# Reload order, head 0's loads first, and key sums on VectorE in a fused linear and softmax attention kernel

## The chip, the cores and the metric

The kernel runs on one core of a Trainium2 chip. The core has five engines that run their own instruction streams and meet only through semaphores: TensorE (PE: matmuls; PEld is its weight load), VectorE (DVE), ScalarE (ACT), GpSimd (POOL) and SyncE (SP, here only an issuer of DMAs). Data lie in DRAM, in SBUF (128 partitions, on the chip) and in PSUM, eight banks of 128 x 512 float32 into which TensorE writes its sums. VectorE and ScalarE read banks; GpSimd works on SBUF tiles alone. DMAs are issued from a queue of SP, of ACT or of POOL. The metric is the device time in microseconds, lower is better.

## The reference

One input x (2048 tokens, width 1024) goes through two attention blocks, and a gate per token mixes their outputs:

```python
x = A_x
g = _sigmoid((x * gate_w).sum(-1, keepdims=True))
a = _A_ref(x, A_wqkv, A_wo)
b = _B_ref(x, B_wqkv, B_wo)
return g * a + (1 - g) * b
```

Block A is linear attention with 32 heads of width 32. With `phi(t) = where(t > 0, t + 1, exp(t)) + 1e-6` it needs for each head the sum over tokens of `phi(k)` times v (`kv`), the plain sum of `phi(k)` over tokens (`z`), and then `phi(q) kv / (phi(q) z)`. Block B is softmax attention with 32 heads of width 32: `softmax(q k / sqrt(32)) v`. Each has its own q, k, v weights (1024 x 3072) and output weights (1024 x 1024).

## The kernel before

**Precision.** Matmul operands are cut into a high part (ScalarE rounds a copy to fp32r) and a low part (the rest, a subtraction). A product is then three matmuls: high x high, high x low, low x high (`three`, L150 to L159). One matmul of 512 columns takes a slot of 0.2275 us in the planner's table.

**First half, products for block B.** The tokens are handled in two halves, J = 0 and J = 1. For each, v's weights are applied first (`v_pass`), then a block of A's keys and B's values (`block`), then eight *quads* (`quad`, f = 0 to 7), each of which makes q or k for two groups of four heads by seven products (a Strassen-like scheme; `PRODUCTS` s = 0 to 6, four blocks of three matmuls each). The cut weights of the quads go round a ring of 13 places in the big tiles 14 to 20; product s of quad f uses entry (7 f + s) modulo 13. For J = 0 the ring is

```python
spots("20a 20b 15a 14a 19a 19b 17b 14b 18a 18b 16a 16b 17a")
```

A quad gives its side work one step after each product: the step behind product s is written out behind that product and ahead of product s + 1. The weights of the next quad are cut in these steps (ScalarE copies at L304, VectorE subtractions at L299).

**v's cut weights** of the first half are stored to DRAM (`wv_d`) and loaded again for J = 1 into the eight places `STARTS[1]` = 19a 19b 17b 18a 18b 14b 16a 16b (k = 0 to 7). `reload_wv` (L822) does this for k = 0 to 5, one per step, from the step behind product 1 of quad 6 on; `change` does k = 6 and 7 in quad 7. Each is two DMAs of 256 KB on ScalarE's queue (L820). ScalarE's stream is in order, so a DMA that waits holds up the copies behind it.

**The heads' stacks.** Scores of block B use stacked operands: a queries' tile (`q_first` for the first 512 tokens, `q_rest` for the other 1536) and a keys' tile (`k_stack`, 2048 tokens). Their rows 0 to 95 are three loads of 32 rows (high, high, low and high, low, high); rows 96 to 127 are set to zero, with ones in two rows of the keys. Heads 0 and 1 are loaded at the end of the first half: `leave` (steps of the last quad of J = 1) calls `load_first`, with the DMAs on POOL's queue and the memsets on POOL. The order is: first block of queries and keys of head 0 (behind product 3), the same of head 1 (behind product 4), then behind product 6 the rest of head 0, and the rest of head 1.

**The main stretch.** From about 563 us on a planner writes one order out by hand. It keeps an estimate of each engine's time (`T`) and picks among four streams: `linear` (block A: units of 24 matmuls; kinds `kv` with 48 units, `q` with 32, `o` with 32), `maxima` (all scores once, VectorE takes the row maxima at L1440), `heads_` (scores again, ScalarE takes the exponentials at L1579, then the product with v at L1726) and `output`. The order on each engine is fixed when the kernel is built; on the chip the engines only wait for each other's semaphores. Banks are taken and given back in the same plan, so a matmul waits for the last reader of its bank.

- *A kv unit* (L1307 on): ScalarE takes v (L1315) and makes the exponentials and the rest (`phi`, L1098 to L1100); `more`, put off to VectorE, joins them into the key features (L1321) and so frees the unit's bank; GpSimd adds the features, 128 x 256, to `zsum` (L1324, L1326), which both lie in SBUF.
- *Weights of the next kind*: `renew` puts a weight block in `next_w`; `split_w` makes the high part on ScalarE (L1047) and the low part, 128 x 512 from two SBUF tiles, on the engine that it is given (L1049), GpSimd.
- *Softmax sums* on GpSimd: it adds the exponentials of a head, 1536 columns at a time or 512 (L1657, L1661); VectorE does the remaining 512 columns in a bank (L1677).
- *The gate*: `gate_step` (L735) asks for a block of x on SyncE's queue, ScalarE scales it (L753) 8 us later by the plan, GpSimd adds it (L759); at the end VectorE turns the sums into the gate (L771 to L773).

SyncE's stream holds nearly all other DMAs, in order: stores of q and k of the quads, the gate's x, v of a head (`load_v`, L1415), and x for the units (`load_half`).

Of the kernel before, what the change touches and what calls it, by code (L numbers as in the profile page):

```python
# [20 lines left out]
DH = 32  # L21
# [29 lines left out]
def kernel(  # L51
# [18 lines left out]
    nc = tc.nc  # L70
    D, S = xT.shape
    H = D // DH
    NK = D // P
    HK = NK // 2
    NT = S // P
    NJ = S // C
# [6 lines left out]
    def f32(ap):  # L83
        return ap.bitcast(F32)
# [46 lines left out]
    zsum = [mid[6][:, i * HC:(i + 1) * HC] for i in range(2)]  # L131
# [31 lines left out]
    def use(eng, cost, *after):  # L163

        T[eng] = max(T[eng], *after, 0.0) + cost
        return T[eng] + LATENCY[eng]
# [14 lines left out]
    def defer(fn, at, cost=0.6, rank=1, prev=None):  # L181
        item = Later(fn, at, cost, rank, prev)
        later.append(item)
        return item
# [86 lines left out]
    def give(b, at=0.0, items=()):  # L271

        held[b] = False
        free[b] = max(free[b], at)
        readers[b].extend(items)

    def both(*times):

        return None if None in times else max(times)
# [39 lines left out]
    KH = NK // 2  # L319
# [462 lines left out]
    def beside(*streams):  # L782

        streams = list(streams)
        while True:
            for s in list(streams):
                next(s, None)
            yield
# [29 lines left out]
    def load_wv_again(k):  # L818
        for p in range(2):
            nc.scalar.dma_start(f32(ring_w(v_ring(1, k), p)), wv_d[k][:, p * C:(p + 1) * C])  # L820

    def reload_wv():  # L822

        for _ in range((QUADS - 2) * NP + 1):
            yield
        for k in range(NK - 2):
            load_wv_again(k)
            yield

# [150 lines left out]
    def split_kv(raw, k):  # L980
        split(wpart(k, 0), wpart(k, 1), raw, nc.vector)
# [4 lines left out]
    def leave():  # L986

        split_kv(raw_a[2], 2)
        split_kv(raw_a[3], 3)
        yield  # L990
        split_kv(raw_a[0], 0)
        split_kv(raw_a[1], 1)
        yield
        for k in range(KH, NK):
            split_kv(raw_b[k - KH], k)
            if 0 < k - KH < 3:
                load_first(k - KH - 1, 0)
            yield
        load_first(0, 1)
        load_first(1, 1)  # L1000

    def load_first(h, part):

        if not part:
            load_q(h, 0, now=nc.gpsimd)
            load_k(h, 0, nc.gpsimd)
        else:
            load_q(h, 1, NJ, nc.gpsimd)
            for j in range(1, NJ):
                load_k(h, j, nc.gpsimd)  # L1010

    T["sp"] = 0.0

# [40 lines left out]
    next_w = deque()  # L1054

    def pump_w(now=False):

        while next_w and (now or coming_w and coming_w[0][1] <= T["pe"]):
            follow, k, mark, eng = next_w.popleft()
            if not coming_w:  # L1060
                more_w(True)
            split_w(*follow, k, *coming_w.popleft(), eng)
            mark.end = w_ready[k]
            if k + LEAD_W < NK:
                later_w.append((*follow, k + LEAD_W))
            more_w(now)
        more_w(now)
# [76 lines left out]
    def keys_alone(n):  # L1144

        while kv_todo and kv_todo[0][0] <= n:
            yield lambda: both(kv_todo[0][1](), bank_at()) if kv_todo else 0.0
            if kv_todo and kv_todo[0][0] <= n:
                use("pe", AV_SWITCH, kv_todo[0][1]())
                keys_now(T["pe"])  # L1150
# [53 lines left out]
    z_end = [0.0, 0.0]  # L1204
# [39 lines left out]
    def linear():  # L1244
        extra = iter(())
        for n, (i, t) in enumerate(units):
            kind, c = chunks[i]
            follow = chunks[i + 1] if i + 1 < len(chunks) else None

            def renew(k):  # L1250

                mark = Later(None, 0.0, 0.0, 0, None)
                w_left[k][:] = [mark]
                next_w.append((follow, k, mark, nc.gpsimd))
                pump_w()

            yield bank_at
# [54 lines left out]
            if kind == "kv":  # L1312
                va = mid[7][:, (n % 2) * HC:(n % 2 + 1) * HC]
                yield from keys_alone(n - 2)
                nc.scalar.copy(va, ps[:, HC:])  # L1315
                use("act", 0.28, T["pe"] + LATENCY["pe"])
                end = phi(ps, e, HC)

                def more(end, c=c, t=t, e=e, ps=ps):
                    pk = e[:, :HC]  # L1320
                    nc.vector.scalar_tensor_tensor(pk, pk, 1.0, ps[:, :HC], op0=ALU.min, op1=ALU.add)  # L1321
                    z_end[c % 2] = use("pool", 0.69, end)
                    if t == 0:
                        nc.gpsimd.tensor_copy(zsum[c % 2], pk)  # L1324
                    else:
                        nc.gpsimd.tensor_add(zsum[c % 2], zsum[c % 2], pk)  # L1326

                todo = [defer(more, end, 0.34)]
                give(b, 0.0, todo)
                keys(n, c, t, e, va, todo)  # L1330
                if t == NT - 1:
                    assert gate_n[0] > NJ * NK
                    extra = chain_of(*(keysum(x) for x in ((0, c) if i == 0 else (c,))))
            elif kind == "q":
                yield from keys_alone(n - 3)
                yield lambda: None if n - 3 not in turned and chunks[units[n - 3][0]][0] == "q" else 0.0
                end = phi(ps, e, C)
                d = dn[n % 2]

                def sums(_, e=e, ps=ps):  # L1340
                    nc.vector.scalar_tensor_tensor(ps, e, 1.0, ps, op0=ALU.min, op1=ALU.add)

                def scaled(_, c=c, ps=ps, r=r):
                    nc.vector.tensor_mul(r, ps, zrep[:, c * C:(c + 1) * C])

                last = []

                def dens(end, r=r, d=d, last=last):
                    nc.vector.tensor_reduce(d, r.rearrange("p (h d) -> p h d", d=DH), AX.X, ALU.add)
                    nc.scalar.add(d, d, eps)  # L1350
                    last[0].at = use("act", 0.2, end)

                def divide(_, t=t, e=e, ps=ps, d=d):
                    nc.vector.reciprocal(d, d)
                    nc.vector.scalar_tensor_tensor(
                        e.rearrange("p (h d) -> p h d", d=DH), ps.rearrange("p (h d) -> p h d", d=DH),
                        g_sb[:, t:t + 1], d.unsqueeze(2).to_broadcast([P, C // DH, DH]),
                        op0=ALU.mult, op1=ALU.mult)

                todo = chain(((sums, 0.63), (scaled, 0.63), (dens, 0.63), (divide, 0.9)), end)  # L1360
                last.append(todo[-1])
                give(b, 0.0, todo)
                tasks.append((lambda todo=todo: None if kv_todo else both(ended(todo + o_left), o_free[(len(turned) + 1) % 2], bank_at()),
                              lambda n=n, c=c, t=t, e=e, todo=todo: queries(n, c, t, e, todo)))
            else:
                res = mid[(7, 10)[n % 2]]
                give(b, use("act", 0.5, T["pe"] + LATENCY["pe"]))
                nc.scalar.copy(res, ps)
                dma(ra_d[t][:, c * C:(c + 1) * C], res)
# [16 lines left out]
    def load_q(h, j, j1=0, now=None):  # L1386

        g, r = divmod(h, 4)
        j1 = max(j + 1, j1)
        q, sl = q_cols(h, j, j1), slice(j * C, j1 * C)  # L1390
        if h < (2 if j else 3):
            nc.gpsimd.memset(f32(q[3 * DH:, :]), 0.0)
        else:
            dma(f32(q[3 * DH:3 * DH + 2, :]), f32(q[3 * DH + 2:3 * DH + 4, :]))
        for b, p in enumerate((0, 0, 1)):
            (now.dma_start if now else dma)(f32(q[b * DH:(b + 1) * DH, :]), qk_d[0][p][g][r * DH:(r + 1) * DH, sl])
        for i in range(j, j1):
            q_ready[h][i] = max(T["pe"] + 8.0, T["sp"] + 5.0)

    def load_k(h, j, now=None):  # L1400

        g, r = divmod(h, 4)
        k = k_stack[h % 2]
        if h < 2 and j == 0:
            nc.gpsimd.memset(f32(k[3 * DH:, :]), 0.0)
            nc.gpsimd.memset(f32(k[3 * DH:3 * DH + 2, :]), 1.0)
        sl = slice(j * C, (j + 1) * C)
        for b, p in enumerate((0, 1, 0)):
            (now.dma_start if now else dma)(f32(k[b * DH:(b + 1) * DH, sl]), qk_d[1][p][g][r * DH:(r + 1) * DH, sl])
        k_ready[h][j] = max(T["pe"] + 6.0, T["sp"] + 4.0)  # L1410

    def v_tile(h):
# [515 lines left out]
    def output():  # L1928
# [55 lines left out]
        for i, (name, n) in enumerate(seq):  # L1984
# [4 lines left out]
            if name == "X21" and n:  # L1989
                load_ra(n + 1)  # L1990

    quad(1, QUADS - 1, beside(leave(), parts))
    assert next(parts, None) is None
    xh_t[2] = sb.tile([P, 2 * HK * P], F32R, name="xh")
    T["sp"] = 0.0
# [124 lines left out]
```

## Time and profile before

| | |
|---|---|
| time, median of three runs | 2838.11 us (2836.34 to 2838.83) |
| the profiled execution: its time, its span | 2837.45 us, 2835.7 us |
| granted TensorE clock, mean | 0.996 |
| busy: PE, DVE, ACT, POOL | 99%, 80%, 59%, 74% |
| busy between 1400 and 1500 us: PE, DVE, ACT, POOL | 99.76, 82.17, 64.01, 97.27 us of 100 |
| largest groups | softmax sums on POOL (L1661) 1641.9 us; maxima on DVE (L1440) 1285.1; exponentials on ACT (L1579) 1156.5 |

How to read it: "PE bank L154 <- DMA big<-wv: 8.0, 1, 8.0" in a list of waits is engine, output and line, who was waited for, then the total in us, the times and the longest. In a timeline a row has the start and the duration in us, the engine ("ACTq" and "SPq" are DMA issues), the line, the operation, output<-inputs and, in brackets, the idle time before and what ended it. A row of windows has the stretch, its length, the busy us of PE, PEld, DVE, ACT and POOL, then TensorE's granted clock, the DMA engines' share and GB/s. In a list of groups the count is followed by busy us, mean ns of one, and the idle time before. A line that gives one source line's instructions has their shortest, median and longest duration in ns.

### The profile page before, as it was taken

The numbers are of one execution on the slowest core, as the hardware profiler recorded it, in microseconds if no ns is written. First come the engines' busy times: TensorE is split into PE (matmuls) and PEld (weight loads), VectorE is DVE, ScalarE is ACT, GpSimd is POOL, SyncE is SP. The second block draws the span as 40 slices with busy tenths as digits, with TensorE's granted clock in tenths as the row PEclk, the third lists the DMA queues.
The fourth block names the chain that finished last, engine by engine and source line by source line (L and its number), as shares of the span: only waits on it lengthen the run. The fifth ranks groups of instructions, "written<-read, shape, count | busy, mean of one in ns | idle before, by whom it ended". The sixth has DMA issues, their size and how long they took to land.

```text
span 2835.7 us, 46700 instructions
## 1 busy us (share of the span) xinstructions
PE 2801.9 (99%) x15784; PEld 2013.6 (71%) x15784; DVE 2267.4 (80%) x3715; ACT 1664.9 (59%) x3167; POOL 2109.6 (74%) x1151
## 2 busy tenths in 40 slices
PE   9998999989999999999999999999999999999999
PEld 8887888876666666676666777676666666676687
DVE  6696759768888888888888877787888888787678
ACT  4333433336676666776666666666767667676622
POOL 0162017468999999999999988998999999999000
PEclk9999999999999999999999999999999999999999
DMA  8587658682443333433334445566544445333774
GB/s 268 174 270 258 202 158 270 222 231 90 103 107 85 86 89 96 114 96 85 85 96 114 142 141 170 172 197 196 168 124 128 128 132 144 101 101 112 261 236 149
DMA packets 391051, 432.77 MB, mean 153 GB/s; under 512 B 105550, under 2 KB 237902, under 8 KB 389020
## 3 DMA queue, kind: packets, MB, share of 16 engines
q1 hardware_dynamic: 366252, 387.69, 45.7%
q0 software_dynamic: 22256, 37.89, 6.2%
q10 hardware_dynamic: 2304, 4.20, 0.4%
q8 instruction: 126, 2.06, 0.3%
q14 instruction: 113, 0.93, 0.1%
HBM read 287.31 MB, written 127.93 MB: 146 GB/s over the span
## 4 chain that ended last, share of the span: by engine, by line
PE 91%; DVE 4%; DMA 3%; ACT 1%; POOL 1%; issue 1%; SPq 0%; ACTq 0%; POOLq 0%; DVEq 0%
PE bank L1726 16%; PE bank L1576 16%; PE bank L1435 15%; PE bank L154 12%; PE bank L157 12%; PE bank L159 12%; PE bank L644 5%; DVE mx L1440 2%; DMA big<-qk 1%; PE bank L1499 1%; ACT big L1579 1%; PE bank L1229 1%; DMA big<-ra 0%; PE bank L1118 0%; DMA big<-big 0%
## 5 line engine op out<-in xcount | busy, mean ns | idle before, releaser
L1661 POOL TENSOR_TENSOR big<-big,big 128x512 f32<-128x512 f32 (+2 forms) x694 | 1641.9, 2370 | 65.4 <-ACT big L1579 19.9
L1440 DVE TENSOR_REDUCE mx<-bank 128x1 f32<-128x512 f32 x2048 | 1285.1, 685 | 282.8 <-PE bank L1435 280.2
L1579 ACT ACTIVATE big<-bank 128x512 f32<-128x512 f32 x2048 | 1156.5, 602 | 349.4 <-PE bank L1576 289.0
L1435 PE MATMUL bank<-big,big 128*128 128x512 f32 x1888 | 743.7, 396 | 13.3 <-DMA big<-qk 7.9
L1576 PE MATMUL bank<-big,big 128*128 128x512 f32 x1888 | 736.2, 396 | 1.0 <-ACT big L1579 0.3
L154 PE MATMUL bank<-big,big 128*128 128x512 f32 x1408 | 552.5, 392 | 10.5 <-DMA big<-wv 8.0
L157 PE MATMUL bank<-big,big 128*128 128x512 f32 x1408 | 551.0, 391 | 0.0
L159 PE MATMUL bank<-big,big 128*128 128x512 f32 x1404 | 549.3, 391 | 1.1 <-DVE big L299 1.1
L1726 PE MATMUL bank<-big,mid 128*32 128x512 f32 x4096 | 454.5, 593 | 0.0
L1576 PEld LDWEIGHTS bank<-big,big 128*128 128x128 f32 x1888 | 353.8, 188 | 125.6 <-issue 45.3
L1435 PEld LDWEIGHTS bank<-big,big 128*128 128x128 f32 x1888 | 355.6, 188 | 101.8 <-DVE mx L1440 12.9
L1726 PEld LDWEIGHTS bank<-big,mid 128*32 128x32 f32 x4096 | 133.4, 110 | 277.4 <-issue 276.0
L154 PEld LDWEIGHTS bank<-big,big 128*128 128x128 f32 x1408 | 265.3, 188 | 71.9 <-DMA big<-wv 8.4
L159 PEld LDWEIGHTS bank<-big,big 128*128 128x128 f32 x1404 | 264.7, 189 | 58.4 <-DVE big L299 2.4
L157 PEld LDWEIGHTS bank<-big,big 128*128 128x128 f32 x1408 | 265.4, 188 | 56.1 <-issue 0.8
L1677 DVE TENSOR_TENSOR bank<-bank,big 128x512 f32<-128x512 f32 x364 | 253.1, 695 | 6.4 <-ACT big L1579 1.4
L304 ACT CAST big<-mid 128x512 fp32r<-128x512 f32 (+1 forms) x169 | 100.2, 618 | 138.6 <-DVE mid L1845 71.7
L299 DVE TENSOR_TENSOR big<-mid,big 128x512 fp32r<-128x512 f32 (+1 forms) x138 | 99.6, 738 | 75.7 <-ACT big L304 75.2
L644 PE MATMUL bank<-big,big 128*128 128x512 f32 x672 | 152.6, 389 | 0.0
L1657 POOL TENSOR_TENSOR big<-big,big 128x1536 f32<-128x1536 f32 (+1 forms) x31 | 132.8, 4285 | 20.4 <-ACT big L1579 20.4
L1734 ACT COPY mid<-bank 128x512 f32<-128x512 f32 x32 | 18.8, 587 | 217.5 <-PE bank L1726 217.5
L644 PEld LDWEIGHTS bank<-big,big 128*128 128x128 f32 x672 | 126.1, 188 | 26.2
(196 smaller groups left out, 2418.9 us busy)
## 6 DMA issues: line engine op xcount, KB each, us to landing
big<-xs SPq DMA_DIRECT2D x202, 256.0 KB
big<-qk SPq DMA_DIRECT2D x690, 64.0 KB
qk<-mid SPq DMA_DIRECT2D x128, 256.0 KB
xh<-xs SPq DMA_DIRECT2D x102, 256.0 KB
big<-oA SPq DMA_DIRECT2D x86, 256.0 KB
xs<-big SPq DMA_DIRECT2D x64, 256.0 KB
oA<-mid SPq DMA_DIRECT2D x64, 256.0 KB
big<-big POOLq DMA_DIRECT2D x50, 256.0 KB, 4.9
```

What stands on the lines that cost most here:

```text
L154: yield nc.tensor.matmul(ps, sh, mh_, start=(kt == 0), stop=False)
L157: yield nc.tensor.matmul(ps, sh, ml_, start=False, stop=(late and last))
L159: yield nc.tensor.matmul(ps, sl, mh_, start=False, stop=last)
L644: nc.tensor.matmul(bank[at + i], x_, w_, start=(kt == u == 0 and not onto), stop=(kt == KH - 1 and u == 2), skip_group_check=onto)
L1435: nc.tensor.matmul(bank[b], q[:, t % TPC * P:(t % TPC + 1) * P], k[:, j * C:(j + 1) * C], start=True, stop=True)
L1440: nc.vector.tensor_reduce(m[:, t, j:j + 1], bank[b], AX.X, ALU.max)
L1576: nc.tensor.matmul(bank[b], k[:, t * P:(t + 1) * P], q_cols(h, j), start=True, stop=True)
L1579: nc.scalar.activation(pr_t[i][:, j * C:(j + 1) * C], bank[b], AF.Exp, scale=SCALE)
L1657: nc.gpsimd.tensor_add(lacc[:, :qp], pr(0)[:, :qp], pr(1)[:, :qp])
L1661: nc.gpsimd.tensor_add(lacc[:, sl], lacc[:, sl], pr(t)[:, sl])
L1677: nc.vector.tensor_add(lacc[:, qp:] if t == NT - 1 else l_b[:, :n], l_b[:, :n], src)
L1726: nc.tensor.matmul(av_b[j * DH:(j + 1) * DH, :], v[:, t, :], pr(t)[:, j * C:(j + 1) * C], start=(t == 0), stop=(t == NT - 1))
```

## The change

Three edits:

1. `reload_wv` takes k in the order 0, 1, 2, 5, 3, 4. Before, k = 3 was written into 18a in the step behind product 4 of quad 6, ahead of product 5, which reads 18a, and k = 4 into 18b ahead of product 6, which reads 18b: these two products read the reloaded blocks. Now each place is written behind the product of quad 6 that reads it.
2. Head 0's queries and keys are loaded as a whole in the step behind product 2 of the last quad, on POOL's queue; head 1's 18 loads are written out behind the quad, on SyncE's queue. The rows 96 to 127 are set behind a tile's loads, for the keys block by block.
3. The key sums (48 instructions) and the low parts of the main stretch's weights (32) go from GpSimd to VectorE. In the plan `more` costs VectorE 0.68 us, in place of 0.34 there and 0.69 on GpSimd; a low part costs 0.6 on VectorE in place of 1.23 on GpSimd.

```diff
-        for k in range(NK - 2):
+        for k in (0, 1, 2, 5, 3, 4):
             load_wv_again(k)
             yield
...
             split_kv(raw_b[k - KH], k)
-            if 0 < k - KH < 3:
-                load_first(k - KH - 1, 0)
+            if k == KH:
+                load_first(0)
             yield
-        load_first(0, 1)
-        load_first(1, 1)
-
-    def load_first(h, part):
-
-        if not part:
-            load_q(h, 0, now=nc.gpsimd)
-            load_k(h, 0, nc.gpsimd)
-        else:
-            load_q(h, 1, NJ, nc.gpsimd)
-            for j in range(1, NJ):
-                load_k(h, j, nc.gpsimd)
+
+    def load_first(h, now=nc.gpsimd):
+        load_q(h, 0, now=now)
+        load_k(h, 0, now)
+        for j in range(1, NJ):
+            load_k(h, j, now)
+        load_q(h, 1, NJ, now)
...
-                next_w.append((follow, k, mark, nc.gpsimd))
+                next_w.append((follow, k, mark, nc.vector))
...
                     nc.vector.scalar_tensor_tensor(pk, pk, 1.0, ps[:, :HC], op0=ALU.min, op1=ALU.add)
-                    z_end[c % 2] = use("pool", 0.69, end)
+                    z_end[c % 2] = end
                     if t == 0:
-                        nc.gpsimd.tensor_copy(zsum[c % 2], pk)
+                        nc.vector.tensor_copy(zsum[c % 2], pk)
                     else:
-                        nc.gpsimd.tensor_add(zsum[c % 2], zsum[c % 2], pk)
-
-                todo = [defer(more, end, 0.34)]
+                        nc.vector.tensor_add(zsum[c % 2], zsum[c % 2], pk)
+
+                todo = [defer(more, end, 0.68)]
...
-        if h < (2 if j else 3):
-            nc.gpsimd.memset(f32(q[3 * DH:, :]), 0.0)
-        else:
+        if h >= (2 if j else 3):
             dma(f32(q[3 * DH:3 * DH + 2, :]), f32(q[3 * DH + 2:3 * DH + 4, :]))
         for b, p in enumerate((0, 0, 1)):
...
+        if h < (2 if j else 3):
+            nc.gpsimd.memset(f32(q[3 * DH:, :]), 0.0)
...
-        if h < 2 and j == 0:
-            nc.gpsimd.memset(f32(k[3 * DH:, :]), 0.0)
-            nc.gpsimd.memset(f32(k[3 * DH:3 * DH + 2, :]), 1.0)
...
+        if h < 2:
+            nc.gpsimd.memset(f32(k[3 * DH:, sl]), 0.0)
+            nc.gpsimd.memset(f32(k[3 * DH:3 * DH + 2, sl]), 1.0)
...
     quad(1, QUADS - 1, beside(leave(), parts))
+    load_first(1, nc.sync)
     assert next(parts, None) is None
```

## The prediction

> **What bounds the kernel now.** First the page's busy times, then the waits of PE.
>
> ```profile
> span 2835.7 us, 46700 instructions
> PE 2801.9 (99%) x15784; PEld 2013.6 (71%) x15784; DVE 2267.4 (80%) x3715; ACT 1664.9 (59%) x3167; POOL 2109.6 (74%) x1151
> PE bank L154 <- DMA big<-wv: 8.0, 1, 8.0
> PE bank L1435 <- DMA big<-qk: 7.9, 2, 7.5
> PE bank L1435 <- DVE mx L1440: 3.4, 1, 3.4
> ```
>
> TensorE is busy for 2801.9 of 2835.7 us. An edit can win only at its pauses, and three of these make 19 us. It can lose wherever it makes TensorE wait. The change touches the first pause with its reloads, the second with its loads, and with its third edit it gives work to VectorE in a stretch where TensorE and VectorE run hand in hand.
>
> **Edit 1, the order of v's reloads.** The view is the timeline around 262 us and the windows beside it.
>
> ```profile
> 257.77 0.98 ACTq L820 DMA_DIRECT2D big<-wv  x2
> 262.52 0.80 PE L154 MATMUL bank<-big,big 128*128 128x512 f32 x1 [7.99 <-DMA big<-wv]
> 264.68 0.63 PE L157 MATMUL bank<-big,big 128*128 128x512 f32 x1
> 265.11 0.63 PE L159 MATMUL bank<-big,big 128*128 128x512 f32 x1
> 268.16 0.69 DVE L513 TENSOR_TENSOR mid<-bank,mid 128x512 f32<-128x512 f32 x1 [7.76 <-PE bank L159]
> 262.00:333.00 71.00, 70.48 (x299) 57.76 (x300) 41.96 (x65) 26.52 (x46) 0.00 (x0) 0.96 0.74 231
> ```
>
> L513 evaluates product 5 of a quad, so the pause stands ahead of product 5, in quad 6 (the next-to-last quad of the first half, J = 0). Its ring place is 18a: index 6 x 7 + 5 = 47, modulo 13 gives 8, and entry 8 of the first ring is 18a. v's fourth reload (k = 3) goes to 18a, too, and is written out one step earlier, behind product 4. (k = 4 and product 6 stand the same way with 18b.) So the product has to wait for that reload: issued at 257.77, it lets TensorE go at 262.52. With the new order the step behind product 4 loads k = 5 into 14b, which product 4 itself was the last to read; 18a follows behind product 5 and 18b behind product 6. No product reads a reloaded place any more, and the 7.99 us go. Behind the pause the matmuls start 0.43 us apart (264.68, 265.11). The mean clock of 0.96 over 71 us means 0.04 x 71 / 0.5 = 5.7 us at half speed, in which 2.8 us are lost; these go as well. What is late next: ScalarE issues these DMAs in order with its copies, as before; v's first reloaded weights are read only after seven more products, and 18a's DMA now waits for a product that ends before ScalarE gets there. **-10.8 us**; at worst 8.0, should the transfers crowd together.
>
> [...]
>
> **Edit 2, the loads of heads 0 and 1.** The second pause is named after a DMA of qk; the weight load of the same matmul names another releaser.
>
> ```profile
> PEld bank L1435 <- DVE mid L1321: 7.9, 1, 7.9
> 587.63 0.72 ACT L753 ACTIVATE mid<-mid,omg_sb 128x512 f32<-128x512 f32 x1 [11.24 <-DMA mid<-in_xT]
> 590.83 0.45 ACT L1100 ACTIVATE bank<-bank,eps 128x256 f32<-128x256 f32 x1
> 591.31 0.42 DVE L1321 SCALAR_TENSOR_TENSOR mid<-mid,bank 128x256 f32<-128x256 f32 x1 [9.32 <-ACT bank L1100]
> 591.79 0.80 PE L1435 MATMUL bank<-big,big 128*128 128x512 f32 x1 [7.46 <-DMA big<-qk]
> 566.06 0.45 SPq L171 DMA_DIRECT2D mid<-in_xT  x1
> 567.45 6.96 SPq L171 DMA_DIRECT2D xh<-xs  x2
> 576.36 2.70 SPq L171 DMA_DIRECT2D mid<-in_xT  x3
> 577.70 1.46 POOL L1396 DMA_DIRECT2D big<-qk  x3
> 570.00:592.00 22.00, 14.47 (x93) 11.39 (x93) 3.26 (x8) 5.72 (x13) 12.04 (x21) 0.92 1.08 246
> ```
>
> The chain is: x for the gate, asked for by SyncE at 576.36, lets ScalarE's L753 start at 587.63; behind it in ScalarE's order stands L1100; then VectorE's L1321 empties a bank; the bank is free at 591.73, and TensorE goes on at 591.79. Head 0's queries and keys are not in this chain, so their earlier arrival wins nothing. Head 1's 18 loads, 12 of which GpSimd issued from 577.70 on, now stand on SyncE's queue ahead of the gate's x. At 0.45 us each (row at 566.06) they put its issue back by 8.1 us. Against this, those 12 loads (nine of 64 KB, three of 192 KB: 1.15 MB) no longer share the DMA engines, which are full in this stretch (share 1.08); at 246 GB/s that is 4.7 us. The memsets, split by blocks, stay on GpSimd, which has nothing waiting for it there. **+3.4 us**, between -4.7 (only the sharing counts) and +8.1 (only the issue counts).
>
> **Edit 3, key sums and low parts on VectorE.** The groups by form between 660 and 1570 us, POOL's and then DVE's:
>
> ```profile
> L1661 POOL TENSOR_TENSOR big<-big,big 128x1536 f32<-128x1536 f32 x150 | 526.1, 3507 | 9.6
> L1661 POOL TENSOR_TENSOR big<-big,big 128x512 f32<-128x512 f32 x178 | 227.9, 1287 | 10.9
> L1657 POOL TENSOR_TENSOR big<-big,big 128x1536 f32<-128x1536 f32 x14 | 59.3, 4235 | 0.0
> L1326 POOL TENSOR_TENSOR mid<-mid,mid 128x256 f32<-128x256 f32 x36 | 29.3, 813 | 6.8 <-ACT big L1579 6.8
> L1049 POOL TENSOR_TENSOR big<-big,big 128x512 fp32r<-128x512 f32 x14 | 17.8, 1290 | 0.0
> L1049 POOL TENSOR_TENSOR big<-mid,big 128x512 fp32r<-128x512 f32 x7 | 8.9, 1290 | 0.0
> L1324 POOL COPY mid<-mid 128x256 f32<-128x256 f32 x2 | 0.8, 395 | 0.0
> L1440 DVE TENSOR_REDUCE mx<-bank 128x1 f32<-128x512 f32 x964 | 597.5, 684 | 135.5 <-PE bank L1435 135.1
> L1321 DVE SCALAR_TENSOR_TENSOR mid<-mid,bank 128x256 f32<-128x256 f32 x38 | 15.8, 415 | 4.1 <-ACT bank L1100 2.1 <-PE bank L154 1.7
> ```
>
> 36 + 2 + 21 = 59 instructions go from POOL to DVE here. By themselves they take 38 x 0.42 (as L1321) + 21 x 0.69 (as L513) = 30 us there, and VectorE idles 135.5 us ahead of its maxima. That idle time hides them, and the planner is told of them (0.68 and 0.6 us); without the cover they would cost the 30.
>
> But all 59 have no operand in a bank. What such VectorE instructions do beside a busy GpSimd is seen in two other places:
>
> ```profile
> 243.54 1.67 POOL L695 TENSOR_TENSOR big<-zrep,big 128x512 fp32r<-128x512 f32 x1
> 244.19 1.57 DVE L490 TENSOR_TENSOR mid<-mid,mid 128x512 fp32r<-128x512 f32 x1
> 653.25 3.48 POOL L1657 TENSOR_TENSOR big<-big,big 128x1536 f32<-128x1536 f32 x1
> 656.81 10.50 POOL L1661 TENSOR_TENSOR big<-big,big 128x1536 f32<-128x1536 f32 x3
> 655.18 1.58 DVE L771 TENSOR_SCALAR g_sb<-g_sb 128x16 f32<-128x16 f32 x1
> 656.80 0.25 DVE L772 RECIPROCAL g_sb<-g_sb 128x16 f32<-128x16 f32 x1
> 657.09 3.19 DVE L773 TENSOR_SCALAR omg_sb<-g_sb 128x16 f32<-128x16 f32 x1
> L490 DVE TENSOR_TENSOR mid<-mid,mid x64: 676/692/2446, 138.2 to 565.0; 128x512 fp32r<-128x512 f32 x64
> ```
>
> L490 has a median of 692 ns; met by GpSimd's L695 (over at 245.21) it takes 1.57 us and ends at 245.76, 0.55 later. L771 ends at 656.76, 0.03 after GpSimd's L1657; L773 ends at 660.28, where the first of the three L1661 (3.5 us each) ends at 660.31. So a VectorE instruction whose inputs all lie in SBUF stands until GpSimd's running one is over. L1321 and the maxima, which read a bank, show nothing of it.
>
> [...]
>
> How much is it? GpSimd is busy almost throughout. An instruction that comes at a random moment meets each kind with its share of the 910 us and then waits half its length: (526.1 x 3.507 + 227.9 x 1.287 + 59.3 x 4.235) / 2 / 910 = 1.31 us; 59 of them 77 us. What passes on to TensorE is read off L771 and L773: beyond 0.25 each (L772) they lost 4.27 us and TensorE waited 3.4, so 0.9 was cushioned. With the first 0.9 us of each wait free, the mean left is, by kinds, 0.578 x 2.607^2 / 7.014 + 0.250 x 0.387^2 / 2.574 + 0.065 x 3.335^2 / 8.47 = 0.66 us; 59 x 0.66 = 39. GpSimd loses 57 us of its 910 and is met 6% less often: -2. Eleven more low parts come after 1570 us, where VectorE has more room; I take +3 of at most 7 (11 x 0.66). The nine key sums before 653 meet little: 0. **+40 us.** Ends: no cushion, 77 + 7 = +84; all absorbed and GpSimd's relief worth something, -5, about what TensorE idles in the eight windows of 100 us from 700 to 1500 (4.4 us; the first and the last of them):
>
> ```profile
> 700.00:800.00 100.00, 99.88 (x681) 66.06 (x683) 84.16 (x147) 68.20 (x134) 96.30 (x52) 1.00 0.44 112
> 1400.00:1500.00 100.00, 99.76 (x652) 64.22 (x644) 82.17 (x144) 64.01 (x126) 97.27 (x45) 1.00 0.33 86
> ```
>
> I take the value that goes by L773, the one place in which this very collision reached TensorE. What is queued behind a standing VectorE instruction are the maxima, for whose banks TensorE waits.
>
> **The sum.** -10.8 + 3.4 + 40 = +32.6 us. The profiled run took 2837.45 us (1.75 beyond its span); that gives **2870 us**. The median of the runs shown, 2838.11, lies 0.7 above that run, which I leave inside the range.
>
> **Rivals.**
> *VectorE's idle time swallows the waits* (faster). For: it idles 135.5 us there, 77 us of waits fit in as a total, and the planner puts the new work where it thinks VectorE idle. Against: the idle time comes in pieces, and TensorE was passed 3.4 of 4.27 us. It decides if the cushion reaches about 3.5 us, the common long GpSimd instruction. Then edit 3 is 0: 2837.45 - 10.8 + 3.4 = **2830**. Chance 0.17.
> *The waits cancel edit 1* (no change). If four fifths of the new instructions fall on GpSimd's 178 short ones, a wait is 0.64 us on average, under the cushion, and a fifth of the 39 is left: 8 us. 2837.45 - 10.8 + 3.4 + 8 = **2838**. Chance 0.11.
> *Edit 1 doesn't do what it says*, since ScalarE issues the new order late enough for another product to wait: 2870 + 10.8 = **2881**. Chance 0.05; for the index sum above is plain.
> *Forecast*: **2870**, own range 2846 to 2908 (the upper end has edit 3 at +78, nearly without cushion). Chance 0.67.
>
> **How the numbers follow.** About 0.2% (5.7 us) is what a measurement of this kernel can tell from no change. Slower: 0.67 + 0.05 = 0.72; within: 0.11; faster: 0.17. The range runs from 2826, under the faster rival, to 2908; outside are 0.06 above (no cushion at all) and 0.05 below.
>
> **What the profile after would show.** Edit 1: no wait for wv in PE's list, and no clock below 1 near 260 us. Edit 2: L753's wait for in_xT about 3 us longer, and the bank's release by L1321 with it. Edit 3: the key sums and low parts on DVE at means near 1.6 and 1.9 us instead of 0.4 and 0.7, many ending with a POOL instruction; PE waits for DVE's maxima by the dozen. I am wrong if those means stay under 0.8 us, or if they are long and PE's waits don't grow.

## The result and the profile after

The changed kernel takes **2945.65 us** (median of four runs, 2945.42 to 2950.07) against 2838.47 us for the kernel before on the same chip: a ratio of 1.0383, 95% interval 1.0365 to 1.0401, or 107.2 us more. In the changed file the lines of the main stretch have moved up by 5: the maxima are L1435 (their matmul L1430), the exponentials L1574 (matmul L1571), the join of the key features L1316, the key sums L1319 and L1321, the low parts L1044, GpSimd's running sums L1656 and its first sum of a head L1652.

The page of the changed kernel, its busy times and its chain:

```profile
span 2943.6 us, 46715 instructions
...
PE 2858.7 (97%) x15784; PEld 2023.1 (69%) x15784; DVE 2395.0 (81%) x3795; ACT 1669.1 (57%) x3167; POOL 2036.3 (69%) x1065
...
PE 83%; DVE 12%; issue 1%; ACT 1%; DMA 1%; POOL 1%; SPq 0%; DVEq 0%; POOLq 0%; ACTq 0%
```

TensorE was idle for 33.8 us before (2835.7 - 2801.9) and is idle for 84.9 now. Of the chain that ended last, VectorE holds 12%; before it was 4%, by this line of the page of before:

```profile
PE 91%; DVE 4%; DMA 3%; ACT 1%; POOL 1%; issue 1%; SPq 0%; ACTq 0%; POOLq 0%; DVEq 0%
```

The list of TensorE's waits shows who:

```profile
PE bank L1430 <- DVE mx L1435: 32.1, 23, 3.5
PE bank L1571 <- DVE mx L1435: 18.5, 13, 3.3
PE bank L767 <- POOL zrep L759: 6.1, 1, 6.1
PE bank L1571 <- DVE mid L1316: 5.3, 1, 5.3
```

The wait for wv is gone, and 36 waits of the scores' matmuls for VectorE's maxima, 50.6 us, stand where there was one of 3.4. The clock shows the other part. First the row of the changed kernel, then that of before:

```profile
core 0: 2943.6 us, clock 0.986
```

```profile
core 0: 2835.7 us, clock 0.996
```

A mean clock of 0.986 loses 0.014 x 2943.6 = 41 us against full speed, before 0.004 x 2835.7 = 11. So of the 107 us some 30 are TensorE's clock, and 51 are TensorE's visible idle time; what is left, some 26 us, lies inside TensorE's busy time. There the starts of the matmuls lie further apart: summed over the trace, the clock's part and the visible pauses taken out, by some 20 us more than before. Which waits, too short for the list, do this is not shown.

The groups of VectorE between 550 and 1900 us, where all 80 moved instructions lie:

```profile
L1435 DVE TENSOR_REDUCE mx<-bank 128x1 f32<-128x512 f32 x1226 | 767.4, 683 | 147.0 <-PE bank L1430 146.0
...
L1321 DVE TENSOR_TENSOR mid<-mid,mid 128x256 f32<-128x256 f32 x45 | 64.6, 1435 | 1.5
L1044 DVE TENSOR_TENSOR big<-big,big 128x512 fp32r<-128x512 f32 x21 | 41.9, 2000 | 12.9 <-ACT big L1042 12.9
...
L1044 DVE TENSOR_TENSOR big<-mid,big 128x512 fp32r<-128x512 f32 x11 | 15.5, 1409 | 7.2 <-ACT big L1042 7.2
...
L1319 DVE COPY mid<-mid 128x256 f32<-128x256 f32 x3 | 6.5, 2179 | 0.1
```

The moved instructions take 64.6 + 41.9 + 15.5 + 6.5 = 128.5 us. By the shortest of each kind they would take 45 x 0.424, 32 x 0.68 and 3 x 0.29 (293 ns, the shortest copy of e12), 41.7 us. So **87 us** of it is standing. And the maxima still follow 147.0 us of idle time, which has not been used up. Over the whole run that idle time fell by only 20 us, though VectorE is busy for 127.6 us more (2395.0 - 2267.4); first the row of before, then that of the changed kernel:

```profile
L1440 DVE TENSOR_REDUCE mx<-bank 128x1 f32<-128x512 f32 x2048 | 1285.1, 685 | 282.8 <-PE bank L1435 280.2
L1435 DVE TENSOR_REDUCE mx<-bank 128x1 f32<-128x512 f32 x2048 | 1285.9, 685 | 262.8 <-PE bank L1430 260.6
```

One such stand in the changed kernel's timeline, with what it does to TensorE:

```profile
1075.48 10.63 POOL L1656 TENSOR_TENSOR big<-big,big 128x1536 f32<-128x1536 f32 x3
...
1078.69 0.42 DVE L1316 SCALAR_TENSOR_TENSOR mid<-mid,bank 128x256 f32<-128x256 f32 x1
1079.14 3.66 DVE L1321 TENSOR_TENSOR mid<-mid,mid 128x256 f32<-128x256 f32 x1
...
1080.15 0.39 PE L159 MATMUL bank<-big,big 128*128 128x512 f32 x1
1082.72 1.28 DVE L1435 TENSOR_REDUCE mx<-bank 128x1 f32<-128x512 f32 x2
1083.45 0.80 PE L1430 MATMUL bank<-big,big 128*128 128x512 f32 x1 [2.92 <-DVE mx L1435]
```

The key sum starts when the join that feeds it is over, and should take 0.42 us (the shortest of the 45 has 424 ns). It stands 3.24 us beside GpSimd's running sums, inside the instruction and behind no semaphore, so here the engines don't meet through semaphores alone; the maxima behind it empty their banks that much later; TensorE runs on for 1.4 us into the banks that it has and then idles 2.92 us. Its next matmul takes 0.80 us in place of 0.39, at half clock (the granted clock is 0.52 from 1083.4 to 1085.0 us).

### The profile page after: what moved, and what is told of

Its sections match the earlier page's. It is cut to its first block, busy times and chain, and to the rows that moved or that the text cites. A ratio compares the mean times of both kernels' runs of the same rounds, so it can differ in the third digit from the quotient of the medians.

```text
span 2943.6 us, 46715 instructions
## 1 busy us (share of the span) xinstructions
PE 2858.7 (97%) x15784; PEld 2023.1 (69%) x15784; DVE 2395.0 (81%) x3795; ACT 1669.1 (57%) x3167; POOL 2036.3 (69%) x1065
## 4 chain that ended last, share of the span: by engine, by line
PE 83%; DVE 12%; issue 1%; ACT 1%; DMA 1%; POOL 1%; SPq 0%; DVEq 0%; POOLq 0%; ACTq 0%
PE bank L1721 15%; PE bank L1571 13%; PE bank L1430 12%; PE bank L154 12%; PE bank L157 11%; PE bank L159 11%; DVE mx L1435 8%; PE bank L644 5%; DVE mid L1321 1%; DVE bank L1672 1%; ACT big L1574 1%; DVE big L1044 1%; PE bank L1494 1%; PE bank L1224 1%; POOL big L1656 0%
## 5 line engine op out<-in xcount | busy, mean ns | idle before, releaser
L1656 POOL TENSOR_TENSOR big<-big,big 128x512 f32<-128x512 f32 (+2 forms) x694 | 1645.0, 2374 | 180.7 <-ACT big L1574 135.4
L1435 DVE TENSOR_REDUCE mx<-bank 128x1 f32<-128x512 f32 x2048 | 1285.9, 685 | 262.8 <-PE bank L1430 260.6
L1574 ACT ACTIVATE big<-bank 128x512 f32<-128x512 f32 x2048 | 1158.7, 603 | 450.8 <-PE bank L1571 388.8
L1430 PE MATMUL bank<-big,big 128*128 128x512 f32 x1888 | 754.6, 405 | 35.5 <-DVE mx L1435 31.0
L1571 PE MATMUL bank<-big,big 128*128 128x512 f32 x1888 | 745.4, 402 | 25.2 <-DVE mx L1435 17.8
L1571 PEld LDWEIGHTS bank<-big,big 128*128 128x128 f32 x1888 | 357.6, 190 | 162.3 <-issue 38.6
L1430 PEld LDWEIGHTS bank<-big,big 128*128 128x128 f32 x1888 | 360.4, 191 | 147.1 <-DVE mx L1435 62.4
L1652 POOL TENSOR_TENSOR big<-big,big 128x1536 f32<-128x1536 f32 (+1 forms) x31 | 122.1, 3940 | 81.4 <-ACT big L1574 81.4
```

Source lines behind the costliest of these rows:

```text
L1430: nc.tensor.matmul(bank[b], q[:, t % TPC * P:(t % TPC + 1) * P], k[:, j * C:(j + 1) * C], start=True, stop=True)
L1435: nc.vector.tensor_reduce(m[:, t, j:j + 1], bank[b], AX.X, ALU.max)
L1571: nc.tensor.matmul(bank[b], k[:, t * P:(t + 1) * P], q_cols(h, j), start=True, stop=True)
L1574: nc.scalar.activation(pr_t[i][:, j * C:(j + 1) * C], bank[b], AF.Exp, scale=SCALE)
L1652: nc.gpsimd.tensor_add(lacc[:, :qp], pr(0)[:, :qp], pr(1)[:, :qp])
L1656: nc.gpsimd.tensor_add(lacc[:, sl], lacc[:, sl], pr(t)[:, sl])
```

## The experiments

Times are given as differences from the kernel before on the same chip. "Cost" below is the difference from the same kernel without the moved instructions.

### One edit at a time

```diff
 e1_order: only
-        for k in range(NK - 2):
+        for k in (0, 1, 2, 5, 3, 4):
 e2_loads: only load_first, its call behind the quad, and the memsets by blocks
 e3_sums: only the key sums and their 0.68 us in the plan
 e4_lows: only
-                next_w.append((follow, k, mark, nc.gpsimd))
+                next_w.append((follow, k, mark, nc.vector))
```

> Before, with edit 1 alone (v's reloads in the order 0, 1, 2, 5, 3, 4). The prediction's term stands if the pause ahead of product 5 and its 5.7 us at half clock go: 10.8 us less, ratio 0.9962. Rival, the transfers crowd and another product or v's pass waits: 0 to 8 us less, and a wait for a DMA or for a cut weight between 250 and 330 us.

Measured 2827.01 us, ratio 0.9960 (0.9945 to 0.9975): **-11.1**. The same stretch of the kernel before has 70.48 us of TensorE and a clock of 0.93; this run has:

```profile
258.00:333.00 75.00, 75.00 (x333) 62.10 (x332) 51.90 (x80) 32.76 (x57) 2.79 (x2) 1.00 0.82 260
```

TensorE is busy for all 75 us and at full clock; no transfer took the place of the one removed.

> Before, with edit 2 alone (head 0's queries and keys loaded whole, head 1's on SyncE's queue). The prediction has +3.4 us (-4.7 to +8.1), ratio 1.0012, with the gate's x later at ScalarE. Rival, head 0's loads do set the second pause: its 7.5 us go, ratio 0.997.

Measured 2836.06 us, ratio 0.9995 (0.9985 to 1.0004): **-2.1**, no difference. In this run's waits of TensorE the pause is still there, now under its real releaser:

```profile
PE bank L1430 <- DVE mid L1316: 8.2, 1, 8.2
PE bank L154 <- DMA big<-wv: 7.1, 1, 7.1
PE bank L1430 <- DVE mx L1435: 3.4, 1, 3.4
```

Head 0's loads, earlier or later, have no part in it. Both terms of the prediction can be found in the traces: the gate's x is asked for 6.8 us later than before (583.17 against 576.36), its way from there to the start of L753 is 4.3 us shorter (6.98 against 11.27), and TensorE goes on 1.6 us later (593.39 against 591.79). The time of the whole kernel doesn't show that delay.

> Before, with the key sums alone on VectorE. Theory L (each of these instructions stands until GpSimd's running one ends, and the wait is passed on to TensorE with hardly a cushion): 48 instructions with a mean of about 1.5 us in place of 0.42, some 50 us of waits, and pauses that drop the clock: +50 to +75 us. Theory C (the prediction's cushion of 0.9 us): +25 us. Theory W (it is VectorE's added work of 48 x 0.42 = 20 us and the changed plan, not the standing): means near 0.42 us, up to +20 us.

Measured 2903.94 us, ratio 1.0231 (1.0216 to 1.0246): **+65.8**. The groups of this run:

```profile
L1326 DVE TENSOR_TENSOR mid<-mid,mid 128x256 f32<-128x256 f32 x45 | 69.2, 1537 | 1.6
```

> Before, with the weights' low parts alone on VectorE. Theory L: 32 instructions, in the run with all edits 1.1 to 1.5 us in the median with up to 4.5, some 27 us of waits beyond 0.68 each; they come in bursts of eight: +25 to +45 us. Theory C: +15 us. Theory W: 32 x 0.68 = 22 us of added work with means near 0.68, up to +22 us. L asks of the last two runs together about the +113 us that the whole change shows beside edit 1.

Measured 2889.62 us, ratio 1.0182 (1.0165 to 1.0199): **+51.5**. The groups of this run:

```profile
L1049 DVE TENSOR_TENSOR big<-big,big 128x512 fp32r<-128x512 f32 x21 | 41.8, 1995 | 11.2 <-ACT big L1047 11.2
...
L1049 DVE TENSOR_TENSOR big<-mid,big 128x512 fp32r<-128x512 f32 x11 | 15.6, 1414 | 4.9 <-ACT big L1047 4.9
```

The four parts add up to -11.1 - 2.1 + 65.8 + 51.5 = 104, near the 107.2 of the whole: the edits hardly depend on each other, and edit 3 alone makes the loss, some 117 us. Both its halves cost nearly what their instructions take on VectorE: 65.8 for 69.2 us of sums (and 3.5 of copies), 51.5 for 57.4 us of low parts.

### Standing or work?

```diff
 e5_reduce, on e3_sums: one input, not two (the key sums are not kept)
-                        nc.vector.tensor_add(zsum[c % 2], zsum[c % 2], pk)
+                        nc.vector.tensor_reduce(dn[1][:, :1], pk, AX.X, ALU.add)
 e6_no_pool, on the changed kernel; e9_order_no_pool, on e1_order
-            nc.gpsimd.tensor_add(lacc[:, sl], lacc[:, sl], pr(t)[:, sl])
```

> The run with the key sums alone on VectorE, in the same order on every engine, but each of the 45 sums is a VectorE reduction of the same feature tile (one SBUF input, the same 256 columns), and the three copies stay on GpSimd. Left out: the key sums themselves, so the linear attention's denominators lack them. Theory L (two SBUF inputs make it stand beside GpSimd): means near 0.4 us and the time of before, 2838 us, at most 8 more. Theory W (the work and the plan): 2904 us, as with the sums.

Measured 2853.79 us, ratio 1.0057 (1.0042 to 1.0072): **+17.3**. All 45 instructions of one source line in this run, shortest, median, longest:

```profile
L1326 DVE TENSOR_REDUCE dn<-mid x45: 419/420/422, 575.5 to 1589.7; 128x1 f32<-128x256 f32 x45
```

As reductions, with one SBUF input, they never stand, though GpSimd is as busy as ever (its running sums of 1536 columns take 559.9 us between 660 and 1680 us, 561.0 before). One SBUF input alone is not what spares them: the copies at L1319 (2.18 us each in the changed kernel) and the gate's L771 and L773 (1.58 and 3.19 us before) have one, too, and stood. The reductions take 48.5 of the 65.8 us away, against 69.2 - 18.9 = 50.3 us of standing in e3. But 17.3 us are left, as much as the 45 x 0.42 = 18.9 us of work: it looks unhidden, though edit 3's order is in this figure, too.

> The changed kernel with GpSimd's running sums of the softmax (the 694 instructions of its largest group) left out, in the same order otherwise, so that VectorE's new instructions meet almost nothing; the softmax denominators lack those terms. Theory L: 2827 us, as before with edit 1 alone, or some us less, with key sums near 0.42 us and low parts near 0.68. Theory W: 2946 us stays.

Measured 2868.20 us, ratio 1.0109 (1.0094 to 1.0124): 75 us less than the changed kernel. The standing is nearly gone (the key sums' line has 424, 425 and 3577 ns as shortest, median and longest), and yet 43 us more than e1's remain. So a control was needed.

> Edit 1 alone, with GpSimd's running sums (line 1661 of before, 694 instructions) left out; the control for the changed kernel without them (2868.2 us). Theory A, leaving them out costs nothing by itself and the 41 us that stayed there belong to edit 3's place in the order and its work: about 2827, like edit 1 alone. Theory B, leaving them out makes a loss of its own, since matmul starts were spread apart there also from 2100 to 2620 us, where edit 3 has hardly an instruction: 2850 or more, and then edit 3 without a busy GpSimd costs only the difference.

Measured 2817.03 us, ratio 0.9931 (0.9917 to 0.9944): -20.0. Theory B falls: leaving the running sums out makes no loss, it wins 9 us. The moved instructions therefore cost 31.8 + 20.0 = 52 us (54 with edit 2's 2.1) in e6, where hardly any of them stands.

### Order, work or standing?

```diff
 e10_plan_only, on e1_order: edit 3's prices in the plan, the instructions still nc.gpsimd
 e12_old_order, on e1_order: the instructions nc.vector, the prices of before
 e13_old_order_no_pool: e12_old_order without GpSimd's running sums
```

> Edit 1 and edit 3's plan (0.68 us and 0.6 us put down to VectorE, nothing to GpSimd), with the key sums and the low parts still issued to GpSimd. Theory A, edit 3's loss is what VectorE does and waits for: the order costs little, 2827 plus or minus 6. Theory B, the order costs the 17 us that were left with one-input reductions, and something for the low parts: 2842 to 2860.

Measured 2856.23 us, ratio 1.0067 (1.0054 to 1.0081): +19.2, 30 us more than e1. Taken alone this would give a quarter of the loss to the order. But GpSimd's work is in that kernel and not in its plan, so the next two were made.

> Edit 1, and the key sums and low parts issued to VectorE, but in the order that the plan before made (0.34 us on VectorE and 0.69 us on GpSimd for a unit, 1.23 us on GpSimd for a low part). Theory A, edit 3's new order costs some 29 us by itself, as its plan with the instructions on GpSimd had it, and the waits and the work cost the rest: 2943 without edit 2, less 29: about 2916. Theory B, those 29 us came from GpSimd's work being left out of that plan, and edit 3's order costs nothing: about 2943. Theory C, the new order helps, since it gives the units the time that they take on VectorE: over 2955.

Measured 2949.82 us, ratio 1.0396 (1.0381 to 1.0412): +112.0, so the moved instructions cost 112.0 + 11.1 = **123 us** in the old order, against 120 (107.2 + 11.1 + 2.1) in the new one. It lies between theory B and theory C: while GpSimd is busy, edit 3's order neither costs nor wins anything that matters, in the net. That e10's 30 us come from its own false prices follows if nothing cancels; it is argued, not shown. The groups of this run:

```profile
L1326 DVE TENSOR_TENSOR mid<-mid,mid 128x256 f32<-128x256 f32 x45 | 67.6, 1503 | 1.6
L1049 DVE TENSOR_TENSOR big<-big,big 128x512 fp32r<-128x512 f32 x21 | 35.4, 1687 | 2.5 <-ACT big L1047 2.4
...
L1049 DVE TENSOR_TENSOR big<-mid,big 128x512 fp32r<-128x512 f32 x11 | 18.4, 1671 | 3.5 <-ACT big L1047 3.4
...
L1324 DVE COPY mid<-mid 128x256 f32<-128x256 f32 x3 | 1.6, 541 | 0.1
```

They sum to 123.0 us, the very cost. That the two agree so well is in part chance, since some 30 us of the cost are the clock's.

> The same, with GpSimd's running sums (694 instructions) left out, so that hardly anything is left to stand behind; the control is edit 1 without the running sums, 2817.0 us. What it takes above that is the price of 30 us of key sums and low parts up to 1570 us, and of the rest after it, on VectorE without standing. Theory A (order 29): 2817 + 22, about 2839. Theory B (order nothing): about 2868, like the changed kernel without the running sums. Theory H, idle time hides the work, as the prediction had it, and the order was all: 2817 to 2822.

Measured 2853.91 us, ratio 1.0057 (1.0040 to 1.0074): +16.1, so 36 us above its control e9. None of the three numbers; it lies between A and B, and H (the work is hidden) is out. The groups of this run:

```profile
L1440 DVE TENSOR_REDUCE mx<-bank 128x1 f32<-128x512 f32 x1294 | 810.3, 681 | 162.6 <-PE bank L1435 161.2
...
L1326 DVE TENSOR_TENSOR mid<-mid,mid 128x256 f32<-128x256 f32 x45 | 22.5, 500 | 1.6
...
L1049 DVE TENSOR_TENSOR big<-big,big 128x512 fp32r<-128x512 f32 x21 | 16.8, 799 | 2.3 <-ACT big L1047 2.1
L1049 DVE TENSOR_TENSOR big<-mid,big 128x512 fp32r<-128x512 f32 x11 | 7.6, 687 | 3.6 <-ACT big L1047 3.4
...
L1324 DVE COPY mid<-mid 128x256 f32<-128x256 f32 x3 | 0.9, 294 | 0.1
```

47.8 us on VectorE cost 36, beside 162.6 us of idle time ahead of the maxima.

Four of these runs (e1, e9, e12, e13) have one and the same order and differ in two things alone, so the plan has no part between them. With GpSimd's running sums the moved instructions cost 123 us, without them 36. The 87 us between are the price of standing, of which e12 has 123.0 - 47.8 = 75 us more; the 36 us are mostly the price of work, 41.7 of the 47.8 us.

The whole account, with the clock's share as (1 - mean clock) x span above that of the control:

| kernel | moved instructions on VectorE, us | their cost, us | of it clock, us | cost / VectorE time |
|---|---|---|---|---|
| e5_reduce (sums, one input) | 18.9 | 17.3 | 3 | 0.9 |
| e13_old_order_no_pool | 47.8 | 36 | 3 | 0.8 |
| e6_no_pool | 52.4 | 54 | 9 | 1.0 |
| e4_lows | 57.4 | 51.5 | 23 | 0.9 |
| e3_sums | 72.7 | 65.8 | 12 | 0.9 |
| e12_old_order | 123.0 | 123 | 30 | 1.0 |
| changed kernel | 128.5 | 120 | 33 | 0.9 |

The mean clocks have three digits, so a clock entry is good to some 3 us. Whether VectorE works or stands makes little difference: **each microsecond more on VectorE in this stretch takes 0.8 to 1.0 us of the kernel's time**. Without the clock's part it is 0.5 to 0.9 us. Not settled is why e6, in the new order, pays 54 us for 52 where e13, in the old one, pays 36 for 48; so beside a GpSimd that is hardly busy (209 us of the 2237 from 563 to 2800 us in e6, 1931 in e1) the order may count.

### The gate: a better kernel

```diff
 e7_gate_act, on e1_order (e11_no3_gate: the same on edits 1 and 2)
-                nc.vector.tensor_scalar_add(g_sb, g_sb, 1.0)
+                nc.scalar.add(g_sb, g_sb, ones[:, :1])
-                nc.vector.tensor_scalar(omg_sb, g_sb, -1.0, 1.0, op0=ALU.mult, op1=ALU.add)
+                nc.scalar.activation(omg_sb, g_sb, AF.Identity, scale=-1.0, bias=ones[:, :1])
 e8_gate_late, on e1_order: the gate's scaling 14 us behind its load in the plan, a block each 3 us
-GATE_STEP, GATE_FROM = 2.0, 4.0
+GATE_STEP, GATE_FROM = 3.0, 4.0
-        gate_busy.append((T["pe"] + 8.0, n, times))
+        gate_busy.append((T["pe"] + 14.0, n, times))
```

> Before with edit 1, and the gate's last two steps of 128 x 16 (the one added, one minus the gate) on ScalarE in place of VectorE. If the 3.4 us pause near 650 us is VectorE standing beside GpSimd in these two, it goes, with the 3.4 us at half clock behind it: 2827 - 3.4 - 1.7 = 2822 us, ratio 0.9943. If it is the maxima's own load, nothing moves: 2827.

Measured 2822.10 us, ratio 0.9945 (0.9931 to 0.9960): 3.2 us beyond e1 on their two chips, which their intervals don't tell apart. TensorE's waits in this run no longer have the one of 3.4 us for the maxima near 660 us, which e1 still has; so it was the gate's two instructions on VectorE that made it.

```profile
PE bank L1435 <- DVE mid L1321: 7.6, 1, 7.6
PE bank L159 <- DVE big L299: 2.0, 1, 2.0
PE bank L1435 <- ACT big L1579: 1.9, 6, 0.5
```

> Before with edit 1, and the gate's scaling on ScalarE planned 14 us behind its load in place of 8, one block every 3 us in place of 2. If the second pause (8.1 us near 575 us, with 10.2 us at half clock) is ScalarE held by the gate's x, it goes: 2827 - 8 - 5 = 2814 us, ratio 0.9915. If it is the queries' and keys' loads, as the row of waits names it, it stays: 2827.

Measured 2856.41 us, ratio 1.0070 (1.0054 to 1.0087): a miss. The windows of this run show why:

```profile
563.00:660.00 97.00, 95.66 (x610) 73.10 (x609) 78.70 (x143) 49.07 (x105) 53.59 (x53) 1.00 0.69 195
660.00:800.00 140.00, 127.60 (x709) 81.51 (x712) 107.84 (x182) 81.23 (x165) 123.83 (x64) 0.95 0.36 95
```

The second pause, the one that edit 2 was near, is gone (95.66 of 97 us busy at full clock, 85.45 at 0.93 in e1), as the chain through the gate's x says. But the new order waits elsewhere: from 660 to 800 us TensorE is idle for 12.4 us, where e1 idles 0.3.

> Edits 1 and 2 with the gate's two last VectorE instructions (lines 771 and 773 of before) on ScalarE, and no edit 3. By the sum of the single runs: 2838.4 - 11.1 - 2.1 - 5 = 2820; if edit 2 is worth nothing beside edit 1, 2822 as without it.

Measured 2820.45 us, ratio 0.9941 (0.9928 to 0.9955), as forecast by the sum. Of the kernels that leave nothing out this is the fastest, 16.6 us under the kernel before; from e7, without edit 2, it can't be told apart.

## Why the prediction was wrong

**Edit 1** was right in mechanism and size: -10.8 forecast, -11.1 measured, the wait and the slow clock behind it both gone.

**Edit 2** was right in that head 0's queries and keys are not in the chain: the pause stayed, released by the join of the key features. Its +3.4 set 8.1 us of longer queue against 4.7 us of lighter transfers; e2's traces have both, 6.8 us of queue against 4.3 us, and TensorE 1.6 us later. But the run measured -2.1, with an interval from about -4 to +1, so the sum's +3.4 is not felt; where it went is open.

**Edit 3** had the right mechanism, and its term was mis-sized: +40 forecast, about 120 measured. By its steps:

- *That the instructions stand until GpSimd's is over*: right for the moved ones, but put too widely. Not every VectorE instruction with all its inputs in SBUF stands: e5's reductions, 419 to 422 ns for all 45, don't. How long: right in total, partly by luck. 77 us of waits were worked out from 660 to 1570 us, where 63 were measured; ahead of that the sum had nothing and 4 came, behind it +3 (at most 7) and 20 came. Together they are the 87 us. The means expected, near 1.6 and 1.9 us, came out as 1.44 for the sums and (41.9 + 15.5) / 32 = 1.79 for the low parts.
- *That the first 0.9 us of each wait is free*: **the step that failed.** It was read off one place, where 4.27 us lost gave 3.4 us of TensorE's wait. The same pair of numbers reads as well as a share, 0.8 of the time lost, and the runs fit a share. Of the 87 us that the moved instructions stood in the changed kernel, 41 lie beyond the first 0.9 us of each wait, just the +40 of the forecast; the other 46 were not free. e3 and e5, in one order, test it without the work: e3 has 52.7 us of waits with the copies', of which 23.6 lie beyond 0.9 us each, and 48.5 us were paid. So do e12 and e13: 75 us more of waits, 87 us more paid.
- *That VectorE's 135.5 us of idle time hide the 30 us of work*: failed too. e13, in an unchanged order, pays 36 us for instructions that hardly stand, and e5 pays 17.3 of 18.9 us for such as never do. The idle time ahead of the maxima is named after TensorE's matmul, and 262.8 of 282.8 us of it are still there in the changed kernel. The likely reading is that VectorE waits there for banks that TensorE fills late, because VectorE emptied them late: the other half of a lock step, not slack. That it can't be used is shown; why is argued.
- *The clock* was not priced for edit 3, though it was for edit 1. It is some 33 us of the 120.
- *The late low parts* were put too low: eleven were expected behind 1570 us, 16 started there and stood 15.8 us. *GpSimd's relief* (-2) is too small to be seen.

With the share in place of the cushion, and the work not hidden, the prediction's own numbers give 0.8 x (77 + 30) = 86 us, and with the clock's 33 us about 119, beside 120 measured. That they meet so well is partly luck: the 107 us leave out what comes behind 1570 us, and the measured share without the clock is (120 - 33) / 128.5 = 0.7. The size of the clock's term is known only from the runs; that long waits bring one could be read from the 0.96 beside edit 1's pause. The range's upper end, 2908, had nearly no cushion but kept the work hidden and the clock at full speed.

**The rivals.** "VectorE's idle time swallows the waits" was the furthest off: of the 128.5 us, the idle time ahead of the maxima took up 20 at most. "The waits cancel edit 1" needed short waits; the mean stand was 87 / 80 = 1.09 us, over all. "Edit 1 doesn't do what it says" is out by e1.

## What to carry to other kernels

An engine's idle time that is named after its partner's instruction, while that partner is 99% busy through a ring of banks, was no slack in this kernel, where a microsecond more on VectorE took 0.8 to 1.0 us: price work added in such a place at one for one until a run says otherwise, and let one run with an instruction that doesn't stand there, as e5's reductions, tell work from waiting. Before work goes from GpSimd to VectorE, ask whether its form is one that stood here (sums and differences of two SBUF inputs, copies, the gate's 128 x 16 steps; the longest took 3.72, 4.46, 3.10 and 3.19 us) and how long GpSimd's instructions beside it are. Cheaper here were ScalarE (the gate in e7, where the wait of 3.4 us went), and a reduction in place of the sums (+17.3 us against +65.8), which e5 shows for the time alone. When a cushion is read off one event, write down both readings, a fixed amount and a share, and keep both in the range.

## What the hardware showed unexpectedly

The stand is exact. In the changed kernel 58 of the 80 moved instructions stood for more than 0.2 us, and those ended 0.28 us (34 sums), 0.55 us (21 low parts) or 0.15 us (3 copies) behind the end of a GpSimd instruction. A burst of low parts therefore falls into step with GpSimd, as in this timeline:

```profile
783.31 18.36 POOL L1656 TENSOR_TENSOR big<-big,big 128x1536 f32<-128x1536 f32 x5
...
790.69 3.82 DVE L1044 TENSOR_TENSOR big<-mid,big 128x512 fp32r<-128x512 f32 x1 [0.94 <-ACT big L1042]
794.43 1.27 DVE L1435 TENSOR_REDUCE mx<-bank 128x1 f32<-128x512 f32 x2
795.63 2.76 DVE L1044 TENSOR_TENSOR big<-big,big 128x512 fp32r<-128x512 f32 x1
798.31 0.68 DVE L1435 TENSOR_REDUCE mx<-bank 128x1 f32<-128x512 f32 x1
798.91 3.32 DVE L1044 TENSOR_TENSOR big<-big,big 128x512 fp32r<-128x512 f32 x1
```

The low parts end at 794.51, 798.39 and 802.23, 3.9 us apart, each one GpSimd instruction later: the first meets it at random, and the next ones, only a maximum or two later, meet the following one near its start and wait 2.1 and 2.6 us, not half its length. GpSimd gives little back: its five instructions take 18.36 us, 3.67 each in place of 3.51.

TensorE's clock fell to half after far shorter pauses than the prediction's 7.99 us. The trace of the changed kernel has 19 stretches at half clock ahead of its end, each of 3.4, 6.8 or 10.2 us and 85 us together; before there were 3, of 24 us together. One of the 19, at 957.18 us, has a single pause of TensorE longer than 0.2 us in the 7 us ahead of it, and that pause is of 1.74 us.
